# The passage between two halves of a gated SSM / attention kernel: K's stores on SyncE's queue, ahead of the loads not needed at once

## The chip, the cores and the metric

The kernel runs on one core of a Trainium2 chip. TensorE (PE) multiplies, VectorE (DVE), ScalarE (ACT) and GpSimd (POOL) do the elementwise work, SyncE (SP) issues most DMAs. A DMA is issued by an instruction in the line of one engine, in that line's order, and is carried by 16 DMA engines that all queues share. The metric is the device time of one execution in microseconds (us), the median of several runs.

## The reference

With x = u of 2048 rows and 448 columns:

```python
g = sigmoid((x * gate_w).sum(-1, keepdims=True))
a = A(x)     # long convolution: K[d, l] = 2 Re sum_n C[d,n] exp(A[d,n] dt[d] l); y = irfft(rfft(u) * rfft(K)); y + u * D_skip
b = B(x)     # 16 heads, 4 segments of 512 rows: causal softmax attention in the segment, mixed by sigmoid(beta)
             # with a recall from a memory M, z that sums phi(k) v and phi(k) over the earlier segments; then @ wo
return g * a + (1 - g) * b
```

## The kernel before

**First half** (`first_half`, L290, with `project`, `transform_u` and `prepare_params` fed in between). The kernel K[d, l] is built in SBUF as `kb`. Beside it `project` makes q and k of all 16 units (unit i is segment i // 4, head group i % 4, four heads each) and stores them to DRAM as QD and KD (L686), v as VD, the recalled memory numerators of segments 1 to 3 as AM (L701), and their denominators, single rows 28, 60, 92, 124 of the same tile, as DM, with one DMA for each row (L703). `transform_u` stores the first step of u's Fourier transform, GU.

**Second half** (`second_half`, L1032). `transform_k` (L472) does the first step of K's Fourier transform in eight rounds. In each, TensorE multiplies slices of `kb` by `s1k` into two PSUM tiles, ScalarE copies both into `gs` (two buffers), and ScalarE's own queue stores `gs` to DRAM as GK (L494). `convolve` (L498) later loads GK and GU in another order (`gk`, `gu`, 32 of each; every `gk` load needs all eight stores), with its constants `cf` and `cb`, and does the second step, the product and the way back.

`attend` (L805) holds the attention steps: `load(i)` (L817) fetches q and k of unit i; `maxima(i)` (L831) has TensorE compute scores and VectorE reduce them in six steps with `tensor_tensor_reduce` (tiles `jk`, `mx`, with the mask `mk`), then writes the negated maxima into q through GpSimd's queue (L863); `weigh(i)` (L866) computes the exponentials PT, of which GpSimd clears the masked part (L893); `values(i)` (L895) loads V and multiplies. `recall(s)` (L934) loads `am` and `dm` of segment s and adds 1e-6 to `dm` (L940). `skip` (L975) loads u again as `xt` and multiplies by `dbc`, the broadcast D_skip, on GpSimd. wo is set to 0 on VectorE and loaded in four DMAs at the start of `attend` (L808 to L813).

`second_half` steps these generators in a fixed order: rounds of `transform_k` with steps of `maxima(0)` between, the first loads of `convolve`, `maxima(1)`, then 16 passes in which `maxima(i+2)`, `weigh(i)`, `values(i-1)` and steps of `convolve` alternate.

TensorE's instructions keep this order. On the other engines, the DMA lines among them, a scheduler orders instructions by when it expects them to be ready, so an instruction can come far ahead of its place in the text. Every DMA of SP's and ACT's lines signals one of eight semaphores, taken in turn, and waits until the DMA that used the same one before has landed. PSUM has three tiles of tag "a" (two banks each) in the second half: a round of `transform_k` takes two, a step of `maxima` one.

Of the kernel before, what the change touches and what calls it, by code (L numbers as in the profile page):

```python
# [11 lines left out]
F32 = mybir.dt.float32  # L12
# [3 lines left out]
AF = mybir.ActivationFunctionType  # L16
# [6 lines left out]
D = 448  # L23
# [448 lines left out]
def transform_k(nc, k, fp):  # L472


    k2 = k.kb.rearrange("p b q -> p (b q)")
    gkv = k.GK.rearrange("k r n d -> (k r) n d")
    for i in range(8):
        gs = fp.tile([128, 4, 4, 112], F32, tag="gs", name="gs", bufs=2)
        pts = [k.ps("a") for jj in range(2)]
        for b in range(2):  # L480
            o = (32 * b + 4 * i) * 112
            for j in range(4):
                r = slice(32 * j, 32 * j + 32)
                k.mm(
                    pts[j // 2][:, j % 2, :448], k.s1k[r, b], k2[r, o : o + 448],
                    start=(b == 0), stop=(b == 1), tile_position=(32 * j, 0),
                )
        for jj in range(2):
            nc.scalar.activation(
                gs[:, :, 2 * jj : 2 * jj + 2].rearrange("p n j q -> p j n q"),  # L490
                pts[jj][:, :, :448].rearrange("p j (n q) -> p j n q", n=4),
                AF.Copy,
            )
        k.adma(gkv[:, 4 * i : 4 * i + 4], gs.rearrange("p n j q -> p n (j q)"))  # L494
        yield


def convolve(nc, k, fp):  # L498

    NC = 32  # L500
    KB = 4
    cf, cb, gk, gu, ks, pr = {}, {}, {}, {}, {}, {}
    rows = lambda t, c: t[2 * c : 2 * c + 2].rearrange("s r n d -> (s r n) d")

    def load(c):
        if c >= NC:
            return
        if c % KB == 0:
            cf[c // KB] = fp.tile([128, KB, 192], F32, tag="cf", name="cf", bufs=2)
            k.dma(cf[c // KB], k.c_fw[:, c : c + KB])  # L510
            cb[c // KB] = fp.tile([128, 2 * KB, 64], F32, tag="cb", name="cb", bufs=2)
            k.dma(cb[c // KB], k.c_bk[:, 2 * c : 2 * c + 2 * KB])
        gk[c] = fp.tile([128, D], F32, tag="gk", name="gk", bufs=4)
        k.dma(gk[c], rows(k.GK, c))
        gu[c] = fp.tile([128, D], F32, tag="gu", name="gu", bufs=4)
        k.dma(gu[c], rows(k.GU, c))

    def second(c, x, o):

        pt = k.ps("a")  # L520
        w = cf[c // KB]
        for s in range(2):
            r = slice(64 * s, 64 * s + 64)
            k.mm(pt[:, s, :D], w[r, c % KB, o : o + 128], x[r], start=True, stop=True)
        return pt[:, :, :D]

    def transform(c):
        pt = second(c, gk.pop(c), 64)
        ks[c] = fp.tile([128, 2, D], F32, tag="ks", name="ks", bufs=3)
        nc.scalar.activation(ks[c], pt, AF.Copy)  # L530

    def product(c):
        pt = second(c, gu.pop(c), 0)
        pr[c] = fp.tile([128, 2, D], F32, tag="pr", name="pr", bufs=3)
        nc.vector.tensor_tensor(pr[c], pt, ks.pop(c), ALU.mult)

    def back(c):

        pt = k.ps("a")
        for i in range(2):  # L540
            for s in range(2):
                k.mm(
                    pt[64 * s : 64 * s + 64, i, :D], cb[c // KB][:, 2 * ((c + i) % KB) + s], pr[c + i][:, s],
                    start=True, stop=True, tile_position=(0, 64 * s),
                )
            pr.pop(c + i)
        bs = fp.tile([128, 2, D], F32, tag="bs", name="bs", bufs=2)
        nc.scalar.activation(bs, pt[:, :, :D], AF.Copy)
        k.adma(k.BB[2 * c : 2 * c + 4].rearrange("(i s) r n d -> (s r n) i d", i=2), bs)

    for c in range(3):
        load(c)
    for c in range(NC + 2):
        load(c + 3)
        if c < NC:
            transform(c)
        yield
        if 1 <= c <= NC:
            product(c - 1)
            yield  # L560
        if c >= 2 and c % 2 == 1:
            back(c - 3)
            yield
# [45 lines left out]
def project(nc, k, pp):  # L609

    act, copy, v = k.act, k.copy, nc.vector
# [82 lines left out]
    def memory(u, ph):  # L694
        s, hg, nm = u
        if nm == 0:
            pn = k.ps("m")
            k.mm(pn, macc[hg], ph, start=True, stop=True)
            am = pp.tile([128, SEG], F32, tag="e", name="am", bufs=2)
            copy(am, pn, AF.Copy)  # L700
            nc.sync.dma_start(k.AM[hg, :, s - 1], am)  # L701
            for j in range(4):
                nc.sync.dma_start(k.DM[s - 1, j : j + 1, hg], am[32 * j + 28 : 32 * j + 29])  # L703
            return
        pt2 = k.ps("m")
        for t in range(4):
            k.tr(pt2[:, 128 * t : 128 * t + 128], ph[:, 128 * t : 128 * t + 128], k.ident)
        yield 0.9
        pkT = pp.tile([128, SEG], F32, tag="e", name="pkT", bufs=2)
        copy(pkT, pt2, AF.Copy)  # L710
        pm = k.ps("m")
        for t in range(4):
            k.mm(
                pm[:, :128], pkT[:, 128 * t : 128 * t + 128],
                V[:, t, 4 * hg : 4 * hg + 4].rearrange("p h e -> p (h e)"),
                start=(t == 0), stop=(t == 3),
            )
        if s == 0:
            v.tensor_tensor(macc[hg], pm[:, :128], k.bm, ALU.mult)
        else:  # L720
            tm = pp.tile([128, 128], F32, tag="tm", name="tm")
            v.tensor_tensor(tm, pm[:, :128], k.bm, ALU.mult)
            v.tensor_tensor(macc[hg], macc[hg], tm, ALU.add)
# [81 lines left out]
def attend(nc, k, ap):  # L805

    v = nc.vector
    wo = ap.tile([128, 4, D], F32, name="wo")  # L808
    v.memset(wo, 0.0)
    for j in range(4):  # L810
        k.dma(
            wo[32 * j : 32 * j + 28], k.wo.rearrange("(g j e) c -> j e g c", j=4, e=28)[j]
        )  # L813
    Q, K, W, Vs, pvss = {}, {}, {}, {}, {}
    last = {}

    def load(i):  # L817
        if i >= 16:
            return
        s, hg = divmod(i, 4)  # L820
        for t, T, src in (("q", Q, k.QD), ("k", K, k.KD)):
            T[i] = ap.tile([128, 2, SEG], F32R, tag=t, name=t + "u", bufs=4)
            k.dma(T[i].bitcast(F32), src[s, hg])

# [196 lines left out]
    def spare(wc):  # L1023

        t = ap.tile([128, 2, SEG], F32R, tag="qk"[wc % 2], name="rest", bufs=4)
        return t[:, :, :D].bitcast(F32)

    k.load, k.maxima, k.weigh, k.values, k.seg_end = load, maxima, weigh, values, seg_end
    k.norm, k.last_end, k.spare = norm, last_end, spare


def second_half(nc, k, ap, tp, fp, fin):  # L1032
# [5 lines left out]
    def step(g):  # L1038
        return next(g, none) is not none
# [5 lines left out]
    ms = {i: k.maxima(i) for i in range(16)}  # L1045
    for r in range(8):
        step(first)
        if r in (3, 5):
            k.load((r - 1) // 2)
        if r >= 2:  # L1050
            step(ms[0])

# [7 lines left out]
        k.dma(k.gt2[64 * h : 64 * h + 64], k.GD.rearrange("(n h w) -> h n w", h=2, w=16)[h])  # L1060
    fp = fp()
    cv = convolve(nc, k, fp)
    for r in range(3):
        step(ms[1])
    step(ms[0])
# [8 lines left out]
    for i in range(16):  # L1074
        k.load(i + 3)
        ahead = ms.get(i + 2, nothing)
        behind = ms.get(i + 1, nothing)
        w = k.weigh(i)
        for r in range(6):
            step(ahead)  # L1080
            step(w)
            if r == 0:
                step(behind)
            if r == 1:
                step(vals)
                step(behind)
                if i % 4 == 0 and i > 0:
                    ends.append(k.seg_end(i // 4 - 1))
                if i == 15:
                    ends.append(k.norm(3, 0, 3, k.pdma))  # L1090
            elif ends and not step(ends[0]):
                ends.pop(0)
                if ends:
                    step(ends[0])
            if i >= 1 and fi is None:
                acc += RATIO
                while acc >= 1.0:
                    acc -= 1.0
                    step(cv)
            if fi is not None and r % 2 == 1:  # L1100
                load_b(n)
                n += 1
        step(w)
        vals = k.values(i)
        step(vals)
        if i == 13:
            for _ in cv:
                pass
            fi = fin()
            load_b, early, late, last = finish(nc, k, fi)  # L1110
        if i == 14:
            for wc in range(6):
                early(wc)
# [21 lines left out]
def gated_mix(ctx, tc, k):  # L1135
# [12 lines left out]
    def tr(*args):  # L1148
        tc.keep_in_program_order(nc.tensor.transpose(*args))  # L1149

    k.mm, k.tr, k.dma = mm, tr, nc.sync.dma_start

    k.adma, k.pdma = nc.scalar.dma_start, nc.gpsimd.dma_start

# [97 lines left out]
    with ExitStack() as st:  # L1252
# [5 lines left out]
        k.mk = ap.tile([128, 512], F32, name="mk")  # L1258
        nc.sync.dma_start(k.mk, k.c_mk)
        k.dbc = ap.tile([128, D], F32, name="dbc")  # L1260
        nc.sync.dma_start(k.dbc, k.D_skip.unsqueeze(0).broadcast_to([128, D]))
        tp, cs = ExitStack(), ExitStack()

        def fourier():
# [43 lines left out]
```

## Time and profile before

| | |
|---|---|
| runs of the kernel before | 1053.49, 1053.63, 1046.73 us; median 1053.49 |
| profiled execution | 1054.63 us, its span 1052.8 us |
| TensorE matmul / weight load busy | 75% / 42% |
| VectorE, ScalarE, GpSimd busy | 53%, 53%, 15% |
| mean granted TensorE clock | 0.818 |
| DMA | 151.35 MB, mean 144 GB/s over the span |

The chain that ended last, followed back from the end, has PE 45%, DVE 17%, DMA 14%, ACT 12%, issue 7%. Busy shares are means over stages with different limits; the passage between the halves lies at about 566 to 650 us of the span. Lines such as L851 are lines of the program before. In views of instructions the columns are start, length, engine, line, operation, tiles, count, and in brackets the idle time before with what ended it; in views of waits they are who waited, for whom, total us, times, longest. Chain pieces give start, length and what.

### The profile page before, as it was taken

The numbers are of one execution on the slowest core, as the hardware profiler recorded it, in microseconds if no ns is written. First come the engines' busy times: TensorE is split into PE (matmuls) and PEld (weight loads), VectorE is DVE, ScalarE is ACT, GpSimd is POOL, SyncE is SP. The second block draws the span as 40 slices with busy tenths as digits, with TensorE's granted clock in tenths as the row PEclk, the third lists the DMA queues.
The fourth block names the chain that finished last, engine by engine and source line by source line (L and its number), as shares of the span: only waits on it lengthen the run. The fifth ranks groups of instructions, "written<-read, shape, count | busy, mean of one in ns | idle before, by whom it ended". The sixth has DMA issues, their size and how long they took to land.

```text
span 1052.8 us, 18763 instructions
## 1 busy us (share of the span) xinstructions
PE 793.4 (75%) x7413; PEld 440.2 (42%) x7413; DVE 558.5 (53%) x1115; ACT 559.0 (53%) x669; POOL 160.6 (15%) x215
## 2 busy tenths in 40 slices
PE   1265677798777798759975268998999899987485
PEld 0152434355444565437642134444444444444231
DVE  6491524346666476775664045555557555571133
ACT  3425556668888688888883123454335344432210
POOL 0401010101111110101110101113122213222300
PEclk9775776779888899879996565798799789888687
DMA  7853252534222234210624944357446555318607
GB/s 203 247 157 97 83 166 74 167 110 142 82 91 91 90 122 137 86 59 28 190 79 150 348 186 152 96 170 232 131 137 215 177 179 189 127 45 330 137 29 218
DMA packets 90858, 151.35 MB, mean 144 GB/s; under 512 B 20619, under 2 KB 60931, under 8 KB 90723
## 3 DMA queue, kind: packets, MB, share of 16 engines
q1 hardware_dynamic: 80818, 130.26, 39.3%
q10 hardware_dynamic: 8480, 18.62, 4.8%
q0 software_dynamic: 1472, 1.27, 0.5%
q8 instruction: 58, 0.95, 0.4%
q14 instruction: 30, 0.24, 0.1%
HBM read 89.95 MB, written 59.78 MB: 142 GB/s over the span
## 4 chain that ended last, share of the span: by engine, by line
PE 45%; DVE 17%; DMA 14%; ACT 12%; issue 7%; SPq 2%; POOL 1%; DVEq 0%; ACTq 0%; POOLq 0%
PE ps_m L1146 18%; PE ps_a L1146 17%; ACT cs L1139 4%; PE ps_pv L1146 4%; DVE jk L851 4%; DVE X L361 4%; PE ps_arg L1146 3%; DVE Y L365 2%; PE ps_k L1146 2%; PE ps_m L1149 2%; DVE Y L366 2%; DMA dm<-DM 2%; ACT EX L1139 2%; DMA dn<-pvs 2%; ACT L1139 1%
## 5 line engine op out<-in xcount | busy, mean ns | idle before, releaser
L851 DVE CUSTOM_DVE_ANT_0 jk<-ps_a,mk 128x512 f32<-128x512 f32 (+3 forms) x256 | 125.0, 488 | 55.1 <-PE ps_a L1146 47.9
L882 ACT ACTIVATE PT<-ps_a 128x1024 f32<-128x1024 f32 (+1 forms) x96 | 84.1, 881 | 94.7 <-PE ps_a L1146 91.3
L327 POOL TENSOR_TENSOR EX<-EX,cab 128x1024 f32<-128x1024 f32 x28 | 53.5, 1912 | 436.0 <-ACT EX L1139 436.0
L1139 ACT ACTIVATE cs<-ps_arg 128x1024 f32<-128x1024 f32 x112 | 108.3, 1020 | 17.2 <-PE ps_arg L1146 15.4
L1146 PE MATMUL ps_m<-xh,w 112*128 112x512 f32 x256 | 101.7, 443 | 11.4 <-DMA w<-WD 7.5
L1146 PE MATMUL ps_k<-Y,X 128*32 128x64 f32 x3584 | 72.1, 242 | 38.8 <-DVE Y L366 38.4
L1146 PE MATMUL ps_a<-qu,ku 32*128 32x384 f32 (+3 forms) x768 | 90.2, 360 | 6.1 <-DVE mx L851 4.7
L361 DVE TENSOR_TENSOR X<-EX,cs 128x1024 f32<-128x1024 f32 x56 | 68.5, 1223 | 40.1 <-ACT cs L1139 28.6
L1146 PEld LDWEIGHTS ps_k<-Y,X 128*32 128x32 f32 x3584 | 62.1, 124 | 60.2 <-DVE Y L366 48.3
L1146 PEld LDWEIGHTS ps_a<-qu,ku 32*128 32x128 f32 x768 | 69.6, 213 | 17.0 <-DVE mx L851 8.8
L1139 ACT ACTIVATE EY<-ps_arg 128x1024 f32<-128x1024 f32 x56 | 56.4, 1029 | 33.9 <-PE ps_arg L1146 33.7
L893 POOL TENSOR_SCALAR_AFFINE_SELECT PT<-PT 128x256 f32<-128x256 f32 (+1 forms) x96 | 46.5, 488 | 165.4 <-ACT PT L882 163.4
L1146 PE MATMUL ps_a<-ku,qu 32*128 32x512 f32 (+3 forms) x256 | 53.8, 464 | 22.9 <-DVE mx L851 21.8
L1146 PEld LDWEIGHTS ps_m<-xh,w 112*128 112x128 f32 x256 | 51.9, 203 | 40.2 <-issue 14.4
L365 DVE TENSOR_TENSOR Y<-EY,cs 128x1024 f32<-128x1024 f32 x56 | 68.3, 1220 | 0.0
L1139 ACT ACTIVATE cs<-cs,bhp 128x1024 f32<-128x1024 f32 x56 | 64.4, 1150 | 1.8
L1146 PEld LDWEIGHTS ps_a<-ku,qu 32*128 32x128 f32 x256 | 25.6, 216 | 89.4 <-DVE mx L851 44.6
L367 DVE SCALAR_TENSOR_TENSOR Y<-EY,cs 128x512 f32<-128x512 f32 x56 | 38.5, 689 | 39.5 <-ACT cs L1139 39.4
L1146 PE MATMUL ps_arg<-ct,lh 48*128 48x512 bf16 x224 | 48.1, 426 | 9.1 <-ACT cs L1139 7.0
L1146 PE MATMUL ps_m<-xl,w 112*128 112x512 f32 x128 | 53.6, 418 | 0.0
L1146 PEld LDWEIGHTS <-lh 48*128 48x128 bf16 x392 | 21.6, 98 | 70.0 <-issue 46.8
L1146 PE MATMUL ps_m<-wo,pvs 128*128 128x448 f32 x96 | 45.6, 625 | 5.9 <-ACT tb L986 4.9
(182 smaller groups left out, 1350.2 us busy)
## 6 DMA issues: line engine op xcount, KB each, us to landing
w<-WD SPq DMA_DIRECT2D x32, 448.0 KB
qu<-QD SPq DMA_DIRECT2D x16, 512.0 KB
ku<-KD SPq DMA_DIRECT2D x16, 512.0 KB
GU<-gs SPq DMA_DIRECT2D x32, 224.0 KB
GK<-gs ACTq DMA_DIRECT2D x8, 896.0 KB
gk<-GK SPq DMA_DIRECT2D x32, 224.0 KB
gu<-GU SPq DMA_DIRECT2D x32, 224.0 KB
BB<-bs ACTq DMA_DIRECT2D x16, 448.0 KB
```

What stands on the lines that cost most here:

```text
L327: nc.gpsimd.tensor_tensor(o, o, cab, ALU.mult)
L361: v.tensor_tensor(X, ex, t[:, :, 0], ALU.mult)
L365: v.tensor_tensor(Y[:, :, :, :32], lo, y[:, :, :, ::-1], ALU.mult)
L366: v.tensor_tensor(Y[:, 0, :, 32:], ey[:, :, 32:], y[:, 0], ALU.mult)
L367: v.scalar_tensor_tensor(Y[:, 1, :, 32:], ey[:, :, 32:], -1.0, y[:, 1], ALU.mult, ALU.mult)
L851: v.tensor_tensor_reduce(junk[:, :n], pt[:, x, o : o + n], k.mk[:, SEG - n :], 1.0, -3e38, ALU.add, ALU.max, mx[:, 3 - t, h : h + 1],)
L882: nc.scalar.activation(PT[:, 2 * hp : 2 * hp + 2, 512 * b : 512 * b + n], pt[:, :, :n], AF.Exp, scale=SCALE)
L893: nc.gpsimd.affine_select(sl, sl, pat, ALU.is_ge, 0.0, base=0, channel_multiplier=-1)
L1139: return tc.keep_in_program_order(nc.scalar.activation(*args, **kw))
L1146: tc.keep_in_program_order(nc.tensor.matmul(*args, **kw))
L1149: tc.keep_in_program_order(nc.tensor.transpose(*args))
```

## The change

- `transform_k`: `gs` has four buffers in place of two; of the two PSUM tiles of a round ScalarE copies one and VectorE the other; the store of GK is issued by SP.
- A mark: `k.mark(x)` remembers a DMA, and every later `k.dma` is told to be issued after the last marked one. Marked are the loads of k of units 0, 1, 2 and the eight stores of GK, so that loads written later in the text stand behind them in SP's line.
- `load(1)` comes after round 1 and `load(2)` after the rounds (before: after rounds 3 and 5). The first loads of `convolve` are a step of their own, taken just before `load(2)`. wo and `dbc` are loaded in the first of the 16 passes.
- The four DM rows of a tile are stored by one DMA.

```diff
@@ transform_k
-        gs = fp.tile([128, 4, 4, 112], F32, tag="gs", name="gs", bufs=2)
+        gs = fp.tile([128, 4, 4, 112], F32, tag="gs", name="gs", bufs=4)
...
         for jj in range(2):
-            nc.scalar.activation(
-                gs[:, :, 2 * jj : 2 * jj + 2].rearrange("p n j q -> p j n q"),
-                pts[jj][:, :, :448].rearrange("p j (n q) -> p j n q", n=4),
-                AF.Copy,
-            )
-        k.adma(gkv[:, 4 * i : 4 * i + 4], gs.rearrange("p n j q -> p n (j q)"))
+            to = gs[:, :, 2 * jj : 2 * jj + 2].rearrange("p n j q -> p j n q")
+            pt = pts[jj][:, :, :448].rearrange("p j (n q) -> p j n q", n=4)
+            if jj == 0:
+                nc.scalar.activation(to, pt, AF.Copy)
+            else:
+                nc.vector.tensor_copy(to, pt)
+        k.mark(k.dma(gkv[:, 4 * i : 4 * i + 4], gs.rearrange("p n j q -> p n (j q)")))
@@ convolve
     for c in range(3):
         load(c)
+    yield
@@ project, memory
-            for j in range(4):
-                nc.sync.dma_start(k.DM[s - 1, j : j + 1, hg], am[32 * j + 28 : 32 * j + 29])
+            nc.sync.dma_start(k.DM[s - 1, :, hg], am.rearrange("(j e) q -> e j q", e=32)[28])
@@ attend
-    v.memset(wo, 0.0)
-    for j in range(4):
-        k.dma(
-            wo[32 * j : 32 * j + 28], k.wo.rearrange("(g j e) c -> j e g c", j=4, e=28)[j]
-        )
+    def load_wo():
+        v.memset(wo, 0.0)
+        for j in range(4):
+            k.dma(
+                wo[32 * j : 32 * j + 28], k.wo.rearrange("(g j e) c -> j e g c", j=4, e=28)[j]
+            )
+        k.dma(k.dbc, k.D_skip.unsqueeze(0).broadcast_to([128, D]))
@@ attend, load
-            k.dma(T[i].bitcast(F32), src[s, hg])
+            x = k.dma(T[i].bitcast(F32), src[s, hg])
+        if i < 3:
+            k.mark(x)
@@ second_half
-        if r in (3, 5):
-            k.load((r - 1) // 2)
+        if r == 1:
+            k.load(1)
...
     cv = convolve(nc, k, fp)
+    step(cv)
+    k.load(2)
...
+        if i == 0:
+            k.load_wo()
@@ gated_mix
+    def dma(*args):
+        if not marks:
+            return nc.sync.dma_start(*args)
+        with tc.issue_after(marks[-1]):
+            return nc.sync.dma_start(*args)
-        nc.sync.dma_start(k.dbc, k.D_skip.unsqueeze(0).broadcast_to([128, D]))
```

The scheduler makes this SP line of it, from the end of the first half on (number of DMAs where more than one): mk, qu and ku of unit 0, GK x2, qu and ku 1, GK x6, qu 2, GD, ku 2, qu and ku 3, wo x2, cf, cb, gk, gt x2, gu, gk, gu, gk, gu, wo x2, dbc, V, gk, gu, cf, cb, xt x4, am, dm, qu and ku 4. Before, it was: mk, dbc, qu 0, ku 0, qu 1, wo x4, ku 1, qu and ku 2, qu and ku 3, V, xt x4, am, dm, GD, cf, gt x2, cb, then gk and gu in turn, with the eight GK stores in ACT's line beside it.

More of the change, by code (lines that the diff above doesn't have):

```diff
@@ L1026, in spare @@
         return t[:, :, :D].bitcast(F32)
+    k.load_wo = load_wo
     k.load, k.maxima, k.weigh, k.values, k.seg_end = load, maxima, weigh, values, seg_end
@@ L1149, in tr, with mark @@
         tc.keep_in_program_order(nc.tensor.transpose(*args))
-    k.mm, k.tr, k.dma = mm, tr, nc.sync.dma_start
+    k.mm, k.tr = mm, tr
+    marks = []
+    def mark(x):
+        marks.append(x.ins)
+    def dma(*args):
[3 more added lines that the diff above has]
+            return nc.sync.dma_start(*args)
+    k.dma, k.mark = dma, mark
     k.adma, k.pdma = nc.scalar.dma_start, nc.gpsimd.dma_start
```

## The prediction

> **What bounds the kernel now.** I read first the page's slices (40 of 26.3 us each), where VectorE falls to 0 in the twenty-third while the DMA engines stand at 9, then the chain of waits around that place, in order of time.
>
> ```profile
> span 1052.8 us, 18763 instructions
> ...
> DVE  6491524346666476775664045555557555571133
> ...
> DMA  7853252534222234210624944357446555318607
> ```
>
> ```profile
> 570.54 11.68 DMA wo<-in_B_wo
> 582.24 12.57 DMA ku<-KD
> 594.83 14.17 DMA dm<-DM
> 609.02 0.03 DVE dm L940
> ```
>
> Columns are start, length, what. For 38.5 us, from 570.5 to 609.0, the kernel's end hangs on transfers alone. The view of waits over 566 to 610 on VectorE, and that over 555 to 665 on all engines, say who stands there.
>
> ```profile
> DVE dm L940 <- DMA dm<-DM: 39.9, 1, 39.9
> ACT gs L489 <- DMA wo<-in_B_wo: 14.2, 1, 14.2
> ```
>
> VectorE stands 39.9 us ahead of one instruction, the 1e-6 added to dm in recall(1), whose result a later step uses, but which comes in VectorE's order before the first maxima. dm's load is the last of SP's line. ScalarE stands too: its first store of K's first step shares a semaphore with a load of wo and is issued only once that has landed. The instructions of VectorE and the issues, from the timeline:
>
> ```profile
> 567.62 1.55 DVE L809 MEMSET wo<- 128x1792 f32 x1 [0.32 <-issue]
> 609.02 0.20 DVE L940 TENSOR_SCALAR dm<-dm 128x64 f32<-128x64 f32 x1 [39.85 <-DMA dm<-DM]
> 609.15 0.69 DVE L851 CUSTOM_DVE_ANT_0 jk<-ps_a,mk 128x512 f32<-128x512 f32 x1
> ...
> 626.75 0.69 DVE L851 CUSTOM_DVE_ANT_0 jk<-ps_a,mk 128x512 f32<-128x512 f32 x1
> ...
> 636.41 0.69 DVE L851 CUSTOM_DVE_ANT_0 jk<-ps_a,mk 128x512 f32<-128x512 f32 x1
> ...
> 646.16 0.43 DVE L851 CUSTOM_DVE_ANT_0 jk<-ps_a,mk 128x256 f32<-128x256 f32 x1
> 566.91 1.18 SPq L703 DMA_DIRECT2D DM<-am  x4
> 594.83 1.70 SPq L939 DMA_DIRECT2D dm<-DM  x1
> 601.96 0.33 ACTq L494 DMA_DIRECT2D GK<-gs  x1
> ```
>
> Maxima of unit 0 begin at 609.15, of unit 1 at 626.75, of unit 2 at 636.41. The row at 646.16 is the second half of unit 2's fifth step; it matters below.
>
> **The change, part by part.** The orders of the two built programs are the decisive view. TensorE's is the same throughout. VectorE's differs in the passage: eight copies of gs come in between the maxima of unit 0, and the dm instruction moves from before unit 0's first maximum to between the two halves of unit 2's fifth step, just ahead of the row at 646.16. It still waits for dm's load, and that load is still last of SP's line, right after am's. So the wait is not removed, it is moved: 36 us of VectorE's work (610 to 646) now comes before it. After it both programs have the same order. The gain is therefore 646.16 less the time at which the new program passes dm, which is the later of (a) VectorE reaching it and (b) dm landing.
>
> (a) VectorE reaching it. The pieces come from these rows:
>
> ```profile
> 567.86 1.73 ACT L489 ACTIVATE gs<-ps_a 128x896 f32<-128x896 f32 x2 [1.26 <-PE ps_a L1146]
> 565.86 1.97 PE ps_a L1146 x16
> 568.83 1.08 PE ps_a L1146 x8
> 662.14 1.09 DVE L535 TENSOR_TENSOR pr<-ps_a,ks 128x896 f32<-128x896 f32 x1
> 509.96 1.07 DVE L387 COPY kb<-ps_k 128x512 f32<-128x512 f32 x1 [2.31 <-PE ps_k L1146]
> ```
>
> VectorE's copy of a gs half has no row: 1.09 us by the product that reads as many elements from PSUM; by the copy of 512 elements written with strides 1.9; I take 1.1, since gs is written in runs of 112. ScalarE's halves take 0.9 each, so both engines together take about 1.1 where ScalarE took 1.73. The first three rounds run 568 to 573. The first maximum needs ku 0, behind mk and qu 0 on the queue: about 573.5. Units 1 and 2 up to the dm place took 636.41 - 626.75 = 9.7 and 646.16 - 636.41 = 9.8, so a step of maxima takes 9.7 / 6 = 1.6. From 573.5 a round is such a step, a copy (1.1) and up to 0.4 for TensorE between: about 3 us. Five rounds and the last step end at about 590. So VectorE reaches dm at about 610 (at 608 if TensorE runs its rounds in 1.08 us, at 613 if the copy costs 1.9).
>
> (b) dm landing. Sizes are in the DMA view of 555 to 665 (number of DMAs, KB each), the rates in the table by stretch (the last three columns: TensorE's granted clock, DMA share, GB/s).
>
> ```profile
> GK<-gs ACTq DMA_DIRECT2D x8, 896.0 KB
> gk<-GK SPq DMA_DIRECT2D x7, 224.0 KB
> gu<-GU SPq DMA_DIRECT2D x5, 224.0 KB
> cf<-in_c_fw SPq DMA_DIRECT2D x2, 384.0 KB
> cb<-in_c_bk SPq DMA_DIRECT2D x2, 256.0 KB
> wo<-in_B_wo SPq DMA_DIRECT2D x4, 196.0 KB
> ...
> 570.00:574.00 4.00, 0.66 (x8) 0.00 (x0) 0.00 (x0) 0.00 (x0) 0.00 (x0) 0.89 0.61 196
> 576.00:586.00 10.00, 1.24 (x10) 0.84 (x12) 0.00 (x0) 1.73 (x2) 0.00 (x0) 0.50 1.06 184
> 586.00:606.00 20.00, 5.95 (x26) 2.11 (x22) 0.00 (x0) 3.45 (x4) 4.38 (x4) 0.59 1.02 405
> 606.00:610.00 4.00, 0.00 (x0) 0.00 (x0) 0.94 (x4) 0.00 (x0) 0.00 (x0) 0.50 0.32 131
> 628.00:636.00 8.00, 3.07 (x12) 1.36 (x10) 7.00 (x30) 0.59 (x1) 0.77 (x1) 0.50 0.92 276
> ```
>
> Before, four of the eight GK stores were issued by 601.96 and shared the engines with dm's line. In the new order all eight stand ahead of dm, and so do two cf, two cb, four gk and four gu; everything else (mk, dbc, qu and ku 0 to 3, wo, V, xt, am) was ahead of it already. Added: 4 x 896 + 2 x 384 + 2 x 256 + 8 x 224 = 6656 KB, 6.8 MB. At 405 GB/s that is 16.8 us. If the gk and gu loads (1.8 MB) run at the 276 of 628 to 636, where they ran before, it is 18.9. I take 17.8. Against it stand idle shares that fill up: at 570 to 574 the engines moved 196 where 405 was possible (2.1 us lost), and from 606 on they ran dry. The new line also starts 0.9 us earlier, since DM takes one store for four. I take 2 of these 3 us: 609.0 + 17.8 - 2 = 625. The stores must come in time for this: at 2.3 us of DMA time each behind 4.2 MB that is queued by 573, the last is due at about 590, and a round every 3 us from 577 gives it at 590. So the engines stay busy, and (b) is later than (a) by 15 us: transfers decide. Bounds: early, the 184 GB/s at 576 to 586 (full share, wo among what was in flight) does not come back: 10 x (1 - 184/405) = 5.5 us less, and 16.8 for 17.8, all 3 for 2: 617. Late, all 9.3 MB behind the stores run at 276 in place of 405, 33.7 for 23.0 us, and no idle share is won: 609 + 16.8 + 10.7 - 2, about 634.
>
> The Trainium skill, "DMA: Bandwidth & Descriptors", section "Specifications", puts a core's HBM limit at about 358 GB/s, which speaks against the change; by it the 6.8 MB would take 19 us and dm would land near 627, but the row of 586 to 606 shows 405 over 20 us, so the row decides.
>
> Other edits. The four single-row stores of DM become one: it saves SP 0.9 us per unit, in the first half beside ScalarE, VectorE and TensorE, which have the chain there; nothing is won but the start above, and nothing lost if the store is slow, for DM is read last. dbc, wo, xt and am/dm move back. Who waits for them: GpSimd's four xt products (4.4 us) now stand between selects of unit 0's PT, and need xt, which lands 2.6 us before dm (am's 1 MB at 405 lies between); 622 + 4.4 and a few selects of 0.4 to 0.6 end them at about 628, before the values of unit 0 (row 653.63), which stood 7.5 us after 646.16, so at 632 in the new time. qu 4 and ku 4 are queued behind dm, as they were issued after 646 before. wo is first read after that. These cost nothing as long as dm itself comes later; without that cover the xt wait alone would cost up to 9 us (values due at 617 or so, selects ended at 626 or so). After the wait the clock is that of 0.50 that the same work had before.
>
> ```profile
> 647.86 0.33 SPq L823 DMA_DIRECT2D qu<-QD  x1
> 653.63 4.42 PE ps_pv L1146 x32
> 600.30 4.38 POOL L980 TENSOR_TENSOR xt<-xt,dbc 128x448 f32<-128x448 f32 x4 [56.68 <-DMA xt<-in_A_u]
> ```
>
> **The sum.** 646.16 - 625.2 (landing and the 0.2 us instruction) = 21 us. The profiled execution took 1054.63 us, 1.8 more than its span of 1052.8; less 21 it is 1033.6. The median of the three runs, 1053.49, lies 1.1 below the profiled one, so I forecast 1033. Its own range is 617 to 634 for the landing: 29 to 12 us, 1025 to 1042.
>
> **The rivals.** A, the loss: stores and loads on one queue hold each other up. Before, GK went through ScalarE's queue beside SP's, and the two together reached 405; now the 7.3 MB of stores stand in the same line as the loads. If a line that mixes both runs at the 184 of 576 to 586, the 19.0 MB from mk to dm take 103 us from 569, dm lands at 674, 28 us after 646: 1082. It decides from 646 on, at a mean below 19.0 MB / 77 us = 247 GB/s. For it: nothing shows why that stretch was slow at full share. Against: wo, not stores, was in flight then, and the stretch in which GK's stores were issued, 586 to 606, was the fast one. The same page, "Issuing engines are not separate DMA queues", has all queues share the same 16 engines and interleave, by which the choice of queue costs nothing; no row here shows stores and loads of such size in one line. B, no difference that counts: only the loads behind the stores run at 184. 9.3 MB take 51 us from 593, dm lands at 645, gain 1: 1053. For it: wo is now split over two places and could slow both. Against: 0.8 MB of wo slowed 10 us, not 50. C, more gain: dm lands before VectorE asks for it at 610. Gain 36: 1017. It needs 19.0 MB in 41 us, 464 GB/s; no stretch shows more than 413.
>
> ```profile
> 574.00:576.00 2.00, 0.00 (x0) 0.00 (x0) 0.00 (x0) 0.00 (x0) 0.00 (x0) 0.50 1.02 413
> ```
>
> **How the numbers follow.** Forecast 0.84, A 0.06, B 0.07, C 0.03. About 1% (10.5 us) is what a measurement of this kernel can tell from no change. Faster: forecast and C, 0.87; same: B, 0.07; slower: A, 0.06. The range is the forecast's own, widened by 5 us towards C and 2 towards B, for what the bounds may miss.
>
> **What would show it.** Right: VectorE's wait for dm shrinks from 39.9 to about 15 us and begins near 610, inside unit 2's maxima; dm lands at 620 to 630; the stores are issued between 570 and 590; the DMA share is 0.9 or more from 571 to 625; the stage from there on is as long as before, to the end. Wrong: a landing of dm after 640, a DMA share below 0.8 between 575 and 590 (the rounds too slow), or a new wait of TensorE for GpSimd's selects at the first values.

## The result

The changed kernel takes 1036.79 us, the median of four runs (1033.79 to 1040.48), against 1050.11 for the kernel before on the same chip (1043.77 to 1053.63). The ratio is 0.9882, 95% interval 0.9839 to 0.9925: 8 to 17 us faster, 1.2%, a little over the 1% that the prediction took as the least that can be told from no change. In a second series, told of below, it was 1033.17 us and the ratio 0.9803 (0.9743 to 0.9863). The forecast was 1033, with a range of 1020 to 1044. Medians are over all runs of a kernel, while ratios leave out its slow ones, up to three of six, so the two can differ by some us.

**The profile after** is that of the slowest of the four runs, 1040.48 us. Its page:

```profile
span 1038.7 us, 18705 instructions
...
DVE  5573344344667766666677663664555555661223
...
DMA  6754242434322123221341895554555454418607
```

The slice in which VectorE stood at 0 and the DMA engines at 9 is gone. The waits of 566 to 640 (who, for whom, total, times, longest) and the instructions of VectorE and TensorE in the timeline show where the stall went:

```profile
DVE dm L947 <- DMA dm<-DM: 11.9, 1, 11.9
POOL xt L987 <- DMA xt<-in_A_u: 10.7, 1, 10.7
PE ps_a L1158 <- DMA ku<-KD: 2.9, 1, 2.9
```

```profile
570.14 2.52 PE L1158 MATMUL ps_a<-kb,s1k 32*128 32x448 f32 x20
579.73 3.36 PE L1158 MATMUL ps_a<-kb,s1k 32*128 32x448 f32 x14
580.54 0.69 DVE L858 CUSTOM_DVE_ANT_0 jk<-ps_a,mk 128x512 f32<-128x512 f32 x1 [2.62 <-PE ps_a L1158]
583.58 1.09 DVE L494 COPY gs<-ps_a 128x896 f32<-128x896 f32 x1 [1.61 <-PE ps_a L1158]
632.05 0.25 DVE L947 TENSOR_SCALAR dm<-dm 128x64 f32<-128x64 f32 x1 [11.86 <-DMA dm<-DM]
632.22 0.41 DVE L858 CUSTOM_DVE_ANT_0 jk<-ps_a,mk 128x256 f32<-128x256 f32 x1
639.12 2.58 PE L1158 MATMUL ps_pv<-PT,V 128*32 128x512 f32 x12
```

The wait for dm has moved to where it was predicted, between the halves of unit 2's fifth step, and shrunk from 39.9 us to 11.9. The matching starts of before:

```profile
565.79 2.77 PE L1146 MATMUL ps_a<-kb,s1k 32*128 32x448 f32 x20
653.56 1.94 PE L1146 MATMUL ps_pv<-PT,V 128*32 128x512 f32 x8
```

I use the first matmul of K's rounds as the zero of the passage. Before, the row behind dm's new place stood at 646.16 - 565.79 = 80.4 us, after it stands at 632.22 - 570.14 = 62.1: the passage is 18.3 us shorter. What follows took 1052.8 - 646.16 = 406.6 us before and 1038.7 - 632.22 = 406.5 after. The spans differ by 14.1 only, because this execution came to the passage 4.35 us later. The work up to there is the same but for DM's stores, and in the second profile of the changed kernel the rounds begin at 566.08, so this is chance. That what follows agrees to 0.1 us is luck too: over all profiles of this document it takes 400 to 413 us. The length of the passage is the steadier measure: in the second profile it is 60.7 us.

The table by stretch (last three columns: granted clock, DMA share, GB/s), behind it a row of before:

```profile
570.00:574.00 4.00, 3.73 (x31) 1.80 (x32) 2.63 (x5) 1.62 (x3) 0.00 (x0) 1.00 0.58 182
574.00:578.00 4.00, 2.77 (x20) 1.09 (x16) 2.65 (x3) 1.83 (x2) 0.00 (x0) 1.00 1.01 313
578.00:588.00 10.00, 7.31 (x40) 5.21 (x40) 3.79 (x9) 0.97 (x2) 0.00 (x0) 0.55 1.02 392
588.00:592.00 4.00, 3.36 (x24) 2.50 (x18) 2.73 (x9) 0.86 (x1) 0.00 (x0) 0.50 0.81 328
592.00:604.00 12.00, 9.14 (x61) 4.18 (x57) 9.39 (x29) 3.34 (x4) 0.00 (x0) 0.93 0.71 258
610.00:612.00 2.00, 1.30 (x10) 0.92 (x10) 1.74 (x6) 0.00 (x0) 0.00 (x0) 0.50 1.07 212
616.00:620.00 4.00, 3.08 (x30) 2.70 (x28) 3.50 (x17) 1.43 (x2) 0.59 (x1) 0.50 0.99 239
620.00:630.00 10.00, 1.25 (x8) 0.67 (x6) 0.19 (x2) 1.22 (x2) 2.50 (x3) 0.50 1.05 381
```

```profile
566.00:570.00 4.00, 3.73 (x32) 1.88 (x36) 2.15 (x4) 2.33 (x4) 0.00 (x0) 0.96 0.37 132
```

At 578 to 588 stores and loads stand mixed in one line and move 392 GB/s. Then the DMA engines are two to three tenths idle until 604: the stores come too late to fill them.

### The profile page after: what moved, and what is told of

The parts are those of the page before. It is cut to its first block, busy times and chain, and to the rows that moved or that the text cites. A ratio compares the mean times of both kernels' runs of the same rounds, so it can differ in the third digit from the quotient of the medians.

```text
span 1038.7 us, 18705 instructions
## 1 busy us (share of the span) xinstructions
PE 795.3 (77%) x7413; PEld 443.4 (43%) x7413; DVE 567.6 (55%) x1123; ACT 552.6 (53%) x661; POOL 162.9 (16%) x215
## 4 chain that ended last, share of the span: by engine, by line
PE 46%; DVE 17%; DMA 13%; ACT 13%; issue 7%; SPq 2%; POOL 1%; DVEq 0%; ACTq 0%; POOLq 0%
PE ps_a L1158 18%; PE ps_m L1158 17%; ACT cs L1151 4%; PE ps_pv L1158 4%; PE ps_arg L1158 4%; DVE X L361 3%; DVE Y L365 2%; PE ps_k L1158 2%; DVE jk L858 2%; DMA dn<-pvs 2%; ACT EX L1151 2%; PE ps_m L1161 2%; DVE Y L366 2%; DVE pr L536 1%; ACT L1151 1%
## 5 line engine op out<-in xcount | busy, mean ns | idle before, releaser
L1151 ACT ACTIVATE cs<-ps_arg 128x1024 f32<-128x1024 f32 x112 | 108.3, 1020 | 19.1 <-PE ps_arg L1158 17.2
L1158 PE MATMUL ps_m<-xh,w 112*128 112x512 f32 x256 | 103.9, 452 | 10.6 <-DMA w<-WD 6.8
L1158 PEld LDWEIGHTS ps_k<-Y,X 128*32 128x32 f32 x3584 | 63.5, 126 | 59.4 <-DVE Y L366 47.6
L1158 PE MATMUL ps_m<-wo,pvs 128*128 128x448 f32 x96 | 44.6, 613 | 6.4 <-ACT tb L993 5.4
```

Of the source, the lines that this page charges most:

```text
L1151: return tc.keep_in_program_order(nc.scalar.activation(*args, **kw))
L1158: tc.keep_in_program_order(nc.tensor.matmul(*args, **kw))
```

## The experiments

Theory 1, the prediction's: the change gained by putting 36 us of VectorE's work ahead of the wait for dm; dm's landing ends the passage, and behind it the xt products are next. Rivals: the gain is in the stores' queue, the buffers, or the two copying engines. Runs of one kernel scatter by 4 to 26 us, so each profile's passage is read as well: from the first matmul of K's rounds to the second half of unit 2's fifth step, 80.4 us before and 62.1 after. There is one profile of each version (two of the changed kernel).

**dm late.** One instruction of VectorE moves, no other engine's order changes.

```diff
+                x_ = v.tensor_tensor_reduce(   # in maxima(i); i == 4: k.late = x_.ins
...
-        v.tensor_scalar(dn, dn, 1e-6, None, ALU.add)
+        if s == 1:
+            with k.behind(k.late):             # tc.issue_after
+                v.tensor_scalar(dn, dn, 1e-6, None, ALU.add)
+        else: ...
```

> The changed kernel with one instruction moved: the 1e-6 added to dm of segment 1 stands behind the last maxima of unit 4 on VectorE, so nothing early waits for dm's load. Measure: from the first matmul of K's rounds to the first matmul of unit 0's values (after: 639.19 - 570.14 = 69.0 us; before: 653.63 - 565.79 = 87.8 us). Theory (the passage ends with a chain of holds, of which dm is the last but not the only one): VectorE's 11.9 us wait goes, but GpSimd's xt products, which wait for xt at about 627.5, still keep the selects of unit 0's weights until about 633 to 635, so the values start about 4 us earlier only: 65 us, and the kernel is about 4 us faster than the changed one. Rival (dm is the only hold): all 11.9 us are won, 57 us, some 12 us faster.

1021.35 us, ratio 0.9652 (0.9594 to 0.9710). That is 1.5 to 2.3% below the changed kernel's two ratios, 16 to 24 us; by the medians it is 12 to 15. By the time it is the rival's 12 us or more, not the theory's 4. From its timelines of TensorE and GpSimd, and, last, VectorE's row that ends the passage:

```profile
563.26 2.62 PE L1164 MATMUL ps_a<-kb,s1k 32*128 32x448 f32 x20
575.07 2.01 PE L1164 MATMUL ps_a<-kb,s1k 32*128 32x448 f32 x16 [0.48 <-ACT gs L492]
615.04 1.94 PE L1164 MATMUL ps_pv<-PT,V 128*32 128x512 f32 x8
618.11 2.21 POOL L993 TENSOR_TENSOR xt<-xt,dbc 128x448 f32<-128x448 f32 x2 [13.90 <-DMA xt<-in_A_u]
623.27 2.78 PE L1164 MATMUL ps_pv<-PT,V 128*32 128x384 f32 x20 [1.06 <-POOL PT L902]
607.65 0.42 DVE L858 CUSTOM_DVE_ANT_0 jk<-ps_a,mk 128x256 f32<-128x256 f32 x1
```

The values begin at 51.8 us (615.04 - 563.26) where the changed kernel had 69.0, and then stand for GpSimd: xt's products hold the selects, as theory 1 said, and most of the values run from 60.0 on. So they run 9 us earlier than in the changed kernel. The passage, which ends on VectorE, is 44.4 us (607.65 - 563.26), 17.7 less than 62.1, where only 11.9 us of waiting were taken away. Part of it is that K's rounds ran at full clock here: 16 matmuls in 2.01 us, against 14 in 3.36 in the row at 579.73 above. Whether that belongs to the program is asked below.

**dm and xt late.** As before, and GpSimd's four products behind unit 2's selects.

```diff
+            with k.behind(k.selected):         # the last select of weigh(2)
                 nc.gpsimd.tensor_tensor(xt, xt, k.dbc, ALU.mult)
```

> The changed kernel with dm's 1e-6 moved as in the run before, and the four xt products of segment 0 on GpSimd put behind unit 2's selects. Theory (dm's and xt's loads together hold the passage): VectorE and the selects both go on, the values start some 11 to 12 us earlier than in the changed kernel: about 57 to 58 us from the first matmul of the rounds, the kernel about 11 us faster than the changed one. Rival (something else then ends last, such as the rounds, K's stores, or the rest of the line on SyncE's queue, qu and ku of unit 4 behind dm among it): the same 65 us as with dm alone, or what is won comes back as a new wait within the next two passes.

1021.76 us, 0.9631 (0.9567 to 0.9695): as fast as with dm late alone. Its waits have no xt left, and the first values run through from 618.12, 51.7 us after its first round:

```profile
618.12 3.93 PE L1170 MATMUL ps_pv<-PT,V 128*32 128x512 f32 x32 [0.84 <-DMA V<-VD]
```

So the hold was there, and its end brings nothing that six runs can show. By the time, neither number was right: dm alone had already brought the 11 us given here for both, and more.

**The kernel before with dm late.** The same edit on the kernel before.

> The kernel before with nothing but dm's 1e-6 moved behind the last maxima of unit 4: the stores stay on ScalarE's queue with two buffers, ScalarE copies both halves, the loads stay in their old order. Theory (the change gained by moving the wait for dm's load behind 36 us of VectorE's work, the order of stores and loads only paid for dm's later landing): most of the gain comes back without the change. VectorE goes on at 569, then the rounds wait for ScalarE's two buffers, whose stores share the queues with the line of loads (issued 576 to 602 before): the rounds end near 612 to 615 in place of 623, about 11 us faster than before. Rival (the gain comes from the stores' queue, buffers and copies): within 2 us of the kernel before, since then the buffers hold the rounds as long as dm did.

1046.86 us (twelve runs), 0.9965 (0.9927 to 1.0003): 4 us, and at most 8. The theory's 11 us lie outside. Its one profile is kinder to the theory: the passage is 70.9 us, 9.5 less than before.

```profile
568.13 2.77 PE L1152 MATMUL ps_a<-kb,s1k 32*128 32x448 f32 x20
639.00 0.42 DVE L851 CUSTOM_DVE_ANT_0 jk<-ps_a,mk 128x256 f32<-128x256 f32 x1
```

VectorE no longer waits for dm; who waits instead (565 to 650):

```profile
DVE jk L851 <- PE ps_a L1152: 42.9, 8, 17.7
PE ps_a L1152 <- ACT gs L489: 24.4, 7, 12.7
ACT gs L489 <- DMA wo<-in_B_wo: 12.9, 1, 12.9
ACT gs L489 <- DMA GK<-gs: 12.2, 2, 7.0
```

VectorE waits for TensorE's scores, TensorE for ScalarE's copies, and ScalarE for its first store's semaphore, last used by a load of wo, and for buffers whose stores have not landed. This is the same stall by another road: a wait of 39.9 us was taken away, and 4 us by the times, 9.5 by the passage, were won. With the two results above: dm's move alone brings 0.4%, the change alone 1.2 to 2.0%, both together 3.5%. The two are worth more together than apart, so each was in part hidden by the other, and theory 1 holds only half: dm was the outer of two covers. How much was hidden is not well known: by the passages, dm's move and the change bring 28 to 29 us apart, and 31 to 37 together in the five versions with dm late compared at the end.

**wo into 128 partitions.** The kernel before, with

```diff
-        k.dma(wo[32 * j : 32 * j + 28], k.wo.rearrange("(g j e) c -> j e g c", j=4, e=28)[j])
+        k.dma(wo[:, j], k.wo[(0, 112, 224, 320)[j] : (0, 112, 224, 320)[j] + 128])
```

> The kernel before with wo loaded as four DMAs into all 128 partitions, 224 KB each, in place of four into 28 partitions, 196 KB each (the rows of wo land in other places, so the last product is another one; the amount of work is the same). Theory (loads into 28 partitions slow everything that is in flight with them): the stretch at 576 to 586 runs near 400 GB/s in place of 184, ku 0 and dm land about 5 us earlier, VectorE's wait for dm is about 35 us in place of 39.9. Rival (that stretch is slow because of something else, such as K's first stores or the start of many DMAs together): it stays near 184 and dm lands as before.

One run, 1043.61 us. The stretch of 184 GB/s, and VectorE's wait:

```profile
576.00:586.00 10.00, 3.35 (x14) 1.21 (x14) 0.00 (x0) 1.73 (x2) 0.00 (x0) 0.50 1.04 413
603.54 0.20 DVE L938 TENSOR_SCALAR dm<-dm 128x64 f32<-128x64 f32 x1 [34.06 <-DMA dm<-DM]
```

413 in place of 184, a wait of 34.06 in place of 39.85: it was wo's loads into 28 partitions each, and not their bytes, of which there are more here (224 KB each in place of 196). What the prediction left open is settled, by one profile.

**The changed kernel again**, unaltered.

> The changed kernel once more, unaltered, on a chip that it shares with the runs beside it. With dm's 1e-6 late (the run of that name) the kernel was 24 us faster than the changed one by the two ratios, where the wait taken away was 11.9 us; in the changed kernel's profile K's rounds took 28.1 us with the clock at 0.5 from 12 to 20 us after the first round, in the other one 22.3 us at clock 1.0, though both programs have the same instructions up to there. Theory (chance: when TensorE stands for ku 0, the clock falls or not): this profile has rounds of 22 to 24 us, dm is passed 55 to 58 us after the first round instead of 62, and the time is 1030 to 1034. Rival (it is in the program): rounds of 28 us again, dm passed at 62 us, 1036 to 1037.

1033.17 us (1021.83 to 1039.34), 0.9803. Its profile has the slow clock again, and the same wait:

```profile
566.08 2.67 PE L1158 MATMUL ps_a<-kb,s1k 32*128 32x448 f32 x20
578.00:586.00 8.00, 6.62 (x36) 4.83 (x36) 5.10 (x14) 1.75 (x2) 0.00 (x0) 0.50 1.02 389
626.59 0.26 DVE L947 TENSOR_SCALAR dm<-dm 128x64 f32<-128x64 f32 x1 [12.02 <-DMA dm<-DM]
```

dm is passed at 60.5 us, the rounds took 26.5: nearer to the rival by the profile (its 62 and 28), and within the theory's 1030 to 1034 by the median. The clock in K's rounds, over all profiles with four buffers and that order, goes with TensorE's first stand for ku 0: 2.94 and 2.47 us in the two profiles of the changed kernel, 2.98 in one of those below, and the clock fell to 0.5; 2.06, 1.05, 2.26 and 1.58 in the other four with dm late, and it stayed at 1.0. Of a kind each, the first profile of the changed kernel and that of the tenth experiment, whose edits lie behind this point:

```profile
579.71 0.79 PE L1158 MATMUL ps_a<-ku,qu 32*128 32x512 f32 x2 [2.94 <-DMA ku<-KD]
```

```profile
578.05 0.50 PE L1171 MATMUL ps_a<-ku,qu 32*128 32x512 f32 x2 [2.26 <-DMA ku<-KD]
```

The two profiles with two buffers don't fit a border between 2.26 and 2.47 us: with a stand of 3.06 the clock fell, but it fell with 2.15 too, where another stand, for ScalarE's copy, came right behind (its profile, of the next experiment):

```profile
579.51 0.50 PE L1158 MATMUL ps_a<-ku,qu 32*128 32x512 f32 x2 [2.15 <-DMA ku<-KD]
582.72 3.55 PE L1158 MATMUL ps_a<-kb,s1k 32*128 32x448 f32 x16 [2.70 <-ACT gs L492]
```

The stand for ku 0 differs between executions with the same orders (2.94 and 2.47), and with dm late, in versions that are alike up to there but for the copies of two, it was 1.05 to 2.98: that the fall comes by chance, as the theory has it, is likely, but no program was seen both with and without it. Whether it comes less often with dm late isn't settled by one profile of each.

**Two buffers in the changed kernel** (`bufs=4` to `bufs=2`, no other order changes).

> The changed kernel with two buffers gs in place of four; every engine's order is the same. Theory (dm's landing ends the passage, the rounds have slack against it): a round now waits for the store of two rounds before, which lands within about 5 us behind qu 1 and ku 1, so the last stores go out 0 to 3 us later, and dm lands as much later: no more than 3 us slower. Rival (the rounds decide, and the four buffers are what the change gained with): stores behind loads in one line land late, each round from the third on waits 2 to 4 us, and the kernel is 10 us or more slower.

1036.85 us, 0.9854 (0.9792 to 0.9916), beside 0.9803 with four on the same chip: 4 us slower by the medians and 5 by the ratios, with overlapping intervals. The profile is clearer:

```profile
ACT gs L492 <- DMA GK<-gs: 9.7, 2, 6.2
634.07 0.24 DVE L947 TENSOR_SCALAR dm<-dm 128x64 f32<-128x64 f32 x1 [11.80 <-DMA dm<-DM]
```

ScalarE now waits 9.7 us for buffers, but VectorE still waits 11.8 us for dm, which lands 63.5 us after the first round (at 570.6), 1.6 to 3 later than in the two profiles with four. That is the theory's "0 to 3".

**dm late, two buffers.**

> The changed kernel with dm's 1e-6 behind unit 4's maxima (as in the first run) and two buffers gs. Theory (with the wait for dm gone, VectorE's and TensorE's own work sets the passage, so what delays a round now delays the end): the rounds take 26 to 30 us in place of 22.3, and the kernel is 3 to 8 us slower than with four buffers, 1024 to 1029. Rival (xt's landing still holds the selects of unit 0 and hides the rounds): within 2 us of 1021.

1029.17 us, 0.9780 (0.9717 to 0.9842), 8 us by the medians and 13 by the ratios above dm late alone. The rounds took 31.3 us. Direction as in the theory, price at its upper end or beyond. So the buffers count as soon as dm's wait is gone. How much is open: the clock fell in this profile and not in that with dm late alone, and against the next experiment's, where it fell too, the passage is 3.5 us longer (53.3 and 49.8).

**dm late, both copies on ScalarE** (the `if jj == 0 ... else` of the diff becomes `nc.scalar.activation` for both).

> The changed kernel with dm's 1e-6 behind unit 4's maxima and both copies of gs on ScalarE, four buffers. VectorE then has 8.7 us less to do among the maxima, ScalarE's two halves take 1.73 us in a row. Theory (a round is bound by VectorE's maxima and copy, 1.6 + 1.1 us, and by TensorE's 2.0 to 3.4): the rounds take about as long, 21 to 24 us, and the kernel is within 2 us of 1021. Rival (copies on two engines are what lets TensorE go on): each round waits 0.9 us longer for its tiles, 7 us in all, and the kernel is 5 to 8 us slower.

1016.69 us, 0.9679 (0.9618 to 0.9740): no difference that can be measured, so the two engines bring nothing that shows in the time. This execution's rounds took 28.2 us, with the clock at 0.5, as long as the changed kernel's 28.1. So it shows what dm's wait is worth without a difference of the clock: its passage is 49.8 us in place of 62.1, 12.3 less for a wait of 11.9.

```profile
560.89 2.52 PE L1161 MATMUL ps_a<-kb,s1k 32*128 32x448 f32 x20
610.67 0.43 DVE L855 CUSTOM_DVE_ANT_0 jk<-ps_a,mk 128x256 f32<-128x256 f32 x1
```

The four profiles with dm late in which the clock stayed at 1.0 have passages of 43.4 to 44.6 us: the slow clock costs some 5 to 6 us more once dm is out of the way. Copies on ScalarE do not lengthen the passage by themselves: the last experiment has them too, and 43.5 us.

**dm late, K's stores on ScalarE's queue.**

```diff
-        k.mark(k.dma(gkv[:, 4 * i : 4 * i + 4], gs.rearrange(...)))
+        k.mark(k.adma(gkv[:, 4 * i : 4 * i + 4], gs.rearrange(...)))
```

> The changed kernel with dm's 1e-6 behind unit 4's maxima, the stores of K's first step back on ScalarE's queue, with four buffers and copies on two engines. Nothing holds the loads back now, and SP's line goes on with wo, V, xt, am and dm ahead of the rest, as in the kernel before. Theory (what the change gains beyond dm is the stores' place ahead of the loads): the stores share the engines with that line from the second round on and land late; each is on one of ScalarE's semaphores and may wait for a load of SP's; the rounds take 35 to 45 us in place of 22 to 28, and the kernel is 8 to 15 us slower than with dm late alone (1029 to 1036). Rival (the four buffers hide the stores' landing wherever they are queued): within 3 us of 1021, or faster, for xt lands earlier and frees the selects.

1040.84 us, 0.9858 (0.9797 to 0.9918): 19 to 22 us slower than with the stores in SP's line, more than the theory's 8 to 15. ScalarE's timeline:

```profile
573.31 0.92 ACT L492 ACTIVATE gs<-ps_a 128x896 f32<-128x896 f32 x1 [1.80 <-PE ps_a L1164]
593.88 0.35 ACTq L495 DMA_DIRECT2D GK<-gs  x1
594.28 0.92 ACT L492 ACTIVATE gs<-ps_a 128x896 f32<-128x896 f32 x1 [20.05 <-DMA dbc<-in_A_D_skip]
```

The first store is issued only when `dbc`, the load that used the same semaphore, far down SP's line, has landed; ScalarE, whose next copy stands behind that issue, is held for 20.05 us with buffers free. In the kernel before the same place cost 14.2. The rounds took 45.0 us. The edit does two things at once: the stores leave SP's line, and the loads of wo, V, xt, am and dm go ahead again (SP issues dm at 593.44, before the first store at 593.88). Which of the two costs more is not told apart. Together with the two runs before it: of the change's parts the stores' place in SP's line, ahead of the loads, counts most, then the buffers, the copies not measurably.

**dm, xt and wo late** (wo's loads in the third of the 16 passes, `dbc` still in the first).

> The changed kernel with dm's 1e-6 and segment 0's xt products late (as in the second run) and wo's four loads in the third of the 16 passes, in SP's line behind the first loads of the second step. Theory (loads into 28 partitions halve the rate of what is in flight with them): the two stretches near 240 to 270 GB/s around the wo pairs go, the first gk and gu land 2 to 4 us earlier, but nothing in the passage waits for them with dm and xt late: 0 to 3 us faster than the second run's 1021.8. Rival (the wait goes elsewhere): no difference, within 2 us.

1018.67 us, 0.9686 (0.9633 to 0.9739). Eight microseconds of the same place, 32 to 40 after the first round, with wo early (first row, the second experiment) and late:

```profile
598.40:606.40 8.00, 6.88 (x40) 4.58 (x40) 5.67 (x19) 2.55 (x3) 1.39 (x3) 0.50 1.02 252
```

```profile
601.00:609.00 8.00, 6.06 (x28) 3.47 (x30) 5.50 (x21) 2.55 (x3) 0.81 (x2) 0.50 0.96 346
```

The rate rises from 252 to 346 GB/s, and the time does not change: nothing waits for it there. Against the second run the medians say 3 us less and the ratios 0.5% more, so the rival.

**dm late, five rounds before unit 0's maxima.**

```diff
-        if r >= 2:
+        if r >= 4:
             step(ms[0])
+    step(ms[0])
+    step(ms[0])
```

> The changed kernel with dm's 1e-6 behind unit 4's maxima, and the maxima of unit 0 starting after the fifth round instead of the third (the two steps left over follow the rounds). TensorE then has rounds to do while ku 0 is on its way. Theory (TensorE's stand of 2.5 to 2.9 us for ku 0 is what drops the granted clock to 0.5 ten us into the passage, in some executions): no such stand, the clock stays at 1.0 through the rounds, they take 17 to 20 us, the stores go out by then, and the time is 3 to 8 us below that with dm late alone, with less scatter. Rival (the clock falls by its own rhythm, or VectorE's maxima set the pace): the rounds end as late or the first maxima as much later, within 3 us of 1021.

1030.69 us (1027.03 to 1031.74), 0.9781 (0.9734 to 0.9828): 9 to 14 us slower than dm late alone, a miss for both. The scatter is gone as the theory said, and the clock fell all the same (575 to 583, a clock of 0.63): without scores to do TensorE ran into the buffers, and stood behind ScalarE's copy.

```profile
ACT gs L492 <- DMA GK<-gs: 6.3, 2, 3.8
575.94 2.62 PE L1166 MATMUL ps_a<-kb,s1k 32*128 32x448 f32 x16 [1.70 <-ACT gs L492]
575.00:583.00 8.00, 6.81 (x38) 3.98 (x38) 4.78 (x10) 1.85 (x3) 0.00 (x0) 0.63 0.99 384
```

So a long stand for ku 0 goes with a fall of the clock but is not needed for it; here 1.70 us for another reason went with it.

**dm, xt and wo late, copies on ScalarE.**

> The version with dm's 1e-6, segment 0's xt products and wo's loads late, and both copies of gs on ScalarE. Theory (with those waits gone the passage is VectorE's and TensorE's work, and copies taken from VectorE shorten it by up to 8.7 us less what ScalarE's longer rounds cost): 1012 to 1017. Rival (the copies have slack on either engine, as the run with one engine and dm late suggests, 1016.7 against 1021.4 with overlapping intervals): 1017 to 1021, no measurable difference from the run before.

1017.52 us, 0.9650 (0.9603 to 0.9697). The rival again. The five versions with dm late that keep the order of the rounds, four buffers and the stores in SP's line lie at 0.963 to 0.969, with upper ends of 0.974 or less: below the changed kernel's 0.9743 to 0.9863 and 0.9839 to 0.9925. None is measurably faster than another.

## Why the prediction was right, and where not

**The wait moves, it is not removed**: right. The gain was to be 646.16 less the time at which dm is passed, and was: 18.3 us in the passage (19.7 in the second profile) against 21 in the sum, nothing behind it. The forecast lies 4 us below one median and at the other. That it is so near is in part luck: the errors under (b) have both signs.

**(a) VectorE at dm**: predicted 44.2 us after the first round (610 - 565.8), measured 50.0 (620.2). Two terms were too small. The first maximum came 10.4 us after the first round (580.54) and not 7.7, since ku 0 landed at 579.6, 6.6 us after its issue at 573.00. And the three rounds behind it took 4.4 to 4.8 us each (the first from 579.73 to 584.49), not 3: I took TensorE's rounds from rows of 1.97 and 1.08 us, while at the clock of 0.5 they take 3.4. That is 7.3 us together, of which the other terms, a little too large, gave 1.5 back. The copy, 1.09, was right.

**(b) dm landing**: predicted 59.2 us after the first round, measured 61.9 and 60.5. The size is nearly right, its parts are not. "The engines stay busy" is wrong, and with it the sign that the stores are issued by 590: the last one went out 30 us after the first round (at 600.0) and not 24 (the late rounds of (a)), and at 588 to 604 shares of 0.81 and 0.71 leave 4.2 us idle. Of the 2 us that I took from filled idle shares, 1.6 came: this passage begins 4.35 us later, so 182 and 313 GB/s at 570 to 578 stand against 132 and 196 at 566 to 574 before, which at 405 is 0.5 and 1.1 us. Against the lull, the slow stretch shrank from 10 us at 184 to two and four at 212 and 239, which at 405 saves 5.5 - 2.6 = 2.9 us. 4.2 + 0.4 - 2.9 gives 1.7 us later; 2.7 and 1.3 were measured. The mean share from 570 to 625 was 0.91, which hides the lull.

**That (b) comes after (a)**: right, by 11.9 us and not 15. This is why the copies' and buffers' price did not matter here.

**The rivals.** A is dead: 392 GB/s with stores and loads in one line at 578 to 588, where the 247 decided. The ScalarE-queue run shows the reverse of A: on a queue of their own, behind a shared semaphore and with the loads ahead again, the stores cost 20 us. B is dead: 381 behind the stores, and the wo run shows what was slow. C is dead as forecast: dm does not land before VectorE comes. (That no stretch had shown more than 413 holds for those of the table; two us of before, 588 to 590, moved 430, still short of the 464 that C needs.) The 358 GB/s that the Trainium skill, "DMA: Bandwidth & Descriptors", section "Specifications", puts as a limit is passed here too, by 392 over 10 us. (By that figure the prediction's sum gives an estimate of 626 for the landing, not the 627 that it names.)

**The cover.** "Without dm's cover the xt wait would cost up to 9 us": the wait is real (13.9 us on GpSimd with dm late), its price in time was not shown: without it the kernel was no faster, within intervals that leave room for several us.

**What the prediction did not see** is that two stalls lay over each other in the passage. It priced the stores' move only as 6.8 MB more ahead of dm, a loss; that store line was itself worth 20 us once dm was out of the way, and the kernel before kept most of its stall when only dm was moved.

What stays open: what drops the granted clock in K's rounds, and whether it drops less often with dm late. Of the 17.7 us by which the passage with dm late is shorter than the changed kernel's, about 12 are the wait and 5 to 6 the clock, by the one profile with dm late in which the clock fell too.

## What to carry to other kernels

When an engine stands for a result that it needs much later, move the instruction that waits, and not only the transfer; but price the move with the next stall in place, because two stalls over the same stretch hide each other, and only a run with both taken away shows what each is worth. Before putting an engine's stores on its own queue, see which semaphore the first of them shares: an issue that waits there holds the engine's next computation, with buffers free. A time for a matmul is to be taken from a row at the clock that the stage will have.

## What the runs showed of the hardware that I had not expected

- Four loads into 28 partitions each slowed everything in flight with them to 184 GB/s at a DMA share of 1.06; loads of more bytes into 128 partitions ran at 413.
- The granted clock fell to 0.5 nine to eleven us into the passage in three of seven profiles with four buffers and the same order of the rounds; the rounds then took 26.5 to 28.2 us in place of 21.4 to 22.6. In those three TensorE first stood 2.47 us or more for ku 0, in the other four 2.26 or less. Stands of 2.15 us (two buffers, another stand right behind) and of 1.70 us (another order) went with a fall too, so the length of one stand does not decide it.
